# A kernel ordered by a planner gets a new model of its transfer queue, a new table of shifts, and another way to write its last block

## The chip, the cores and the metric

The kernel runs on one core of a Trainium2 chip. The metric is the device time of one execution in microseconds (us). TensorE (PE) does the matmuls, ScalarE (ACT) and VectorE (DVE) the work on vectors, GpSimd (POOL) and SyncE (SP) here mostly issue transfers, which sixteen DMA engines carry out. Each engine works through its own list of instructions in order and waits on semaphores for the others.

## The reference

An attention with cosine-weighted ReLU features, without a softmax, and behind it a two-layer network with a squared ReLU. There are 8 batches, 8 heads, 576 positions and a head size of 64; the network has 512 inputs, 2048 hidden values and 512 outputs.

```
def phi(x, c, s):                       # c, s: cos and sin of pi/2 * position / 576
    r = np.maximum(x, 0.0)
    return np.concatenate([r * c, r * s], axis=-1)
q_p, k_p = phi(q, cos_w, sin_w), phi(k, cos_w, sin_w)
kv  = np.einsum('bhsf,bhsd->bhfd', k_p, v)
num = np.einsum('bhsf,bhfd->bhsd', q_p, kv)
den = np.einsum('bhsf,bhf->bhs', q_p, np.sum(k_p, axis=2))[..., None] + 1e-06
x   = (num / den) -> [8 * 576, 512]
h   = x @ moe_w_in;  r = np.maximum(h, 0.0);  g = r * r
out = g @ moe_w_out                     # float32 [4608, 512]
```

## The kernel before, in words

Of each batch's 576 positions, 512 are worked on as four blocks of 128 (`j` = 0 to 3), and the last 64 are kept as a tail: the tails of all eight batches are put together to a ninth block of 512 rows, which goes through the network last (`b == B`, B = 8).

For a batch `b` the work is this. Two 1 MB loads bring q and k (`ldq`, `ldk`, into `kq`), two of 512 KB v (`ldv`, into `vs`), and small ones the tails (`kqt`, `vst`). ScalarE or VectorE make the features (`cos`, `sin`, into `fe`; of the tails into `fet`, of which there is one buffer). TensorE makes `kz`, the product of features and v. The features of q are transposed: of batches 0 and 1 on TensorE, of the later ones by a DMA transpose on SP's queue (`qTd`: `qpT<-fe` twice and `qpTt<-fet` once for each batch). TensorE makes `num`, VectorE divides (`div`, into `xp`), and the result is transposed again (`xTd`: `xT<-xp` twice and `xTt<-xpt` once). Then come the first layer (`hps` where it is a plain product, in the blocks 0 to 2; `ha`, `hb`, `hc` where it is a product of two by two blocks in seven products P1 to P7 instead of eight, in blocks 3 to 8), the squared ReLU (`rt`, then `gT`), and the second layer (`plan_pair`: `ya`, `yb`, again seven products, with sums `gs` on VectorE; block 0 in `plan_first2`). A store of 512 KB for each half of a block takes it to memory on SP's queue.

The first 17 us are written out by hand (`begin`). All that follows are operations of a planner (`Plan`, lines 133 to 355): each has a cost in us on one engine or on either of ScalarE and VectorE, the operations that it comes after, and the buffers that it holds. `timeline` sets due times along TensorE's work, `dues` carries them back to what it needs, and `run` simulates the engines: at each moment an engine takes the ready operation with the smallest key, which is the due time plus an entry of the table `SHIFT`. `PINS` fixes some operations to one engine. `EARLY`, `EARLY_TAIL`, `STRETCH` and `BIAS` are further settings. The order that comes out is the order in which the instructions are emitted; nothing of the simulation is left at run time, when only the lists and the semaphores count. So whatever changes the planner's figures changes the order on every engine, SP's queue among them.

A transfer ends, for the planner before, by one running time for all transfers (lines 319 to 324), to which a margin `CARE` is added:

```
before, service, behind = o.done
dma = max(dma, free[e] + before) + service
o.end = dma + behind + CARE
```

The last block's second layer (`plan_pair(B, True)`, line 1176 on) has three PSUM buffers of 512 columns: `ya`, `yb` and `yc`. TensorE's order at the end is P1, P5, P6, P3, P7, P2, P4, where P2 adds to `ya` and P4 to `yb`; each is then copied into a half of `y`. The tail block's rows lie in memory in runs of 64, one for each batch. `store` (line 1110) writes one such run from 64 partitions of `y`, 128 KB, and `plan_store` makes eight of these.

## Time and profile before

| | |
|---|---|
| median of 3 runs | 287.29 us (286.31 to 289.38) |
| the profiled execution's own time | 288.8 us |
| span of its instructions | 286.3 us |
| busy: TensorE, VectorE, ScalarE | 269.6, 220.2, 201.0 us |
| granted TensorE clock, mean | 0.986 |
| transfers | 53.0 MB, 185 GB/s over the span |
| last matmul's end; last store's landing; end of the span | 279.6; 285.3; 286.3 us |

The span runs from the first instruction of the profiled execution to its last. A row of a timeline has the start and the length in us, the engine (with a q: its sequencer, which issues transfers), the line, the operation, what it writes and reads, the shapes, how many there were, and in brackets how long the engine had stood idle before it, with what ended that. PEld is TensorE's loading of weights. Lines such as L535 are those of helpers that many operations share, so the tiles tell the work apart.

### The profile page before, as it was taken

How to read it: one execution, taken by the hardware profiler on the slowest of the kernel's cores; microseconds unless marked ns; L12 is line 12 of the kernel's file. 1: busy time of each engine (PE TensorE's matmuls, PEld its weight loads, DVE VectorE, ACT ScalarE, POOL GpSimd, SP SyncE). 2: the span in 40 equal slices, each digit the busy share in tenths (PEclk: the TensorE clock that was granted, in tenths of full speed). 3: DMA queues.
4: the chain of work that ended last, by engine and by line, in shares of the span. 5: the costliest groups of instructions: out<-in, count | busy, mean ns of one | idle time of the engine just before them, and what ended most of it. 6: DMA issues, size and time to landing. Idle time of an engine off the chain costs nothing.

```text
span 286.3 us, 6926 instructions
## 1 busy us (share of the span) xinstructions
PE 269.6 (94%) x2835; PEld 227.5 (79%) x2835; DVE 220.2 (77%) x423; ACT 201.0 (70%) x337; POOL 29.0 (10%) x46
## 2 busy tenths in 40 slices
PE   8999999999979889899988999999999999999990
PEld 3579765888869769788876889988988888888880
DVE  1779658998964988799986997999985956966810
ACT  3769983698398596798559996977675866776510
POOL 8834661100000000000000000000000000000000
PEclk9999999999999999999997999999999999999996
DMA  6999999858999999999994799369511101101106
GB/s 235 310 207 308 319 250 338 269 145 233 342 181 221 262 299 176 294 234 261 242 269 124 185 253 303 137 165 167 36 41 76 74 2 73 76 0 76 72 3 147
DMA packets 77502, 53.00 MB, mean 185 GB/s; under 512 B 52096, under 2 KB 72576, under 8 KB 77472
## 3 DMA queue, kind: packets, MB, share of 16 engines
q1 hardware_dynamic: 70448, 38.81, 55.0%
q0 software_dynamic: 7024, 13.76, 18.4%
q8 instruction: 22, 0.36, 0.6%
q14 instruction: 8, 0.07, 0.1%
HBM read 36.70 MB, written 9.44 MB: 161 GB/s over the span
## 4 chain that ended last, share of the span: by engine, by line
PE 71%; DMA 16%; ACT 4%; SPq 2%; issue 2%; POOL 2%; DVE 1%; POOLq 0%; ACTq 0%
PE ya L535 13%; PE hps L535 12%; PE yb L535 12%; PE hb L535 10%; PE hc L535 6%; PE ha L535 6%; DMA kq<-in_q_dram 5%; PE yh L535 5%; DMA qpT<-fe 4%; DMA kq<-in_k_dram 3%; DMA qpTt<-fet 3%; PE num L535 2%; PE kz L535 2%; SPq L691 1%; ACT fe L522 1%
## 5 line engine op out<-in xcount | busy, mean ns | idle before, releaser
L535 PEld LDWEIGHTS <-w1sb 128*128 128x128 bf16 x800 | 74.1, 98 | 11.1 <-issue 2.5
L516 ACT ACTIVATE gT<-rt 128x512 bf16<-128x512 bf16 x93 | 57.8, 630 | 12.7 <-DVE rt L529 10.2
L535 PEld LDWEIGHTS <-gs 128*128 128x128 bf16 x512 | 50.4, 99 | 8.2 <-issue 1.9
L535 PEld LDWEIGHTS <-gT 128*128 128x128 bf16 x448 | 43.2, 98 | 12.5 <-ACT gT L516 1.5
L535 PE MATMUL hps<-xT,w1sb 128*128 128x256 bf16 (+1 forms) x416 | 45.4, 264 | 1.6 <-DMA xT<-xp 1.6
L522 ACT ACTIVATE fe<-kq,cols 128x1024 bf16<-128x1024 f32 (+1 forms) x35 | 35.1, 1044 | 2.5 <-DMA kq<-in_q_dram 2.0
L535 PE MATMUL ya<-w2sb,gT 128*128 128x256 bf16 x256 | 30.6, 273 | 1.7 <-ACT gT L516 1.3
L535 PEld LDWEIGHTS <-w1s 128*128 128x128 bf16 x288 | 27.6, 98 | 3.8 <-issue 0.6
L524 DVE TENSOR_SCALAR fe<-kq,cols 128x1024 bf16<-128x1024 f32 (+1 forms) x37 | 24.7, 710 | 6.3 <-DMA kq<-in_k_dram 5.4
L535 PE MATMUL hb<-xs,w1sb 128*128 128x256 bf16 x192 | 28.6, 276 | 0.9 <-ACT u L506 0.9
L518 DVE TENSOR_TENSOR gT<-rt 128x512 bf16<-128x512 bf16 x51 | 20.9, 418 | 4.5 <-ACT rt L510 4.2
L535 PE MATMUL ha<-xT,w1sb 128*128 128x256 bf16 x160 | 24.1, 273 | 0.0
L661 DVE TENSOR_TENSOR xp<-num,den 128x512 bf16<-128x512 f32 (+1 forms) x33 | 22.3, 675 | 1.1
L510 ACT ACTIVATE rt<-hps 128x512 bf16<-128x512 f32 x34 | 19.9, 591 | 3.5 <-PE hps L535 2.9
L532 DVE TENSOR_TENSOR gs<-gT 128x2048 bf16<-128x2048 bf16 x16 | 19.5, 1218 | 1.1 <-ACT gT L516 1.0
L529 DVE CUSTOM_DVE_ANT_0 rt<-hb,s 128x512 bf16<-128x512 f32 x24 | 16.4, 684 | 3.1 <-PE hb L535 2.1
L529 DVE CUSTOM_DVE_ANT_0 rt<-hc,u 128x512 bf16<-128x512 f32 x24 | 16.3, 682 | 3.2 <-PE hc L535 3.2
L535 PE MATMUL yb<-w2sb,gs 128*128 128x256 bf16 x128 | 16.3, 284 | 1.6 <-ACT yu L506 1.6
L506 ACT COPY u<-hb 128x512 f32<-128x512 f32 x23 | 13.4, 581 | 4.5 <-PE hb L535 4.5
L506 ACT COPY hb<-ha 128x512 f32<-128x512 f32 x24 | 14.0, 583 | 2.8 <-PE ha L535 1.4
L535 PE MATMUL yb<-w2t,gs 128*128 128x256 bf16 x128 | 15.3, 273 | 0.0
L535 PE MATMUL yb<-w2t,gT 128*128 128x256 bf16 x128 | 15.3, 273 | 0.0
(114 smaller groups left out, 402.4 us busy)
## 6 DMA issues: line engine op xcount, KB each, us to landing
out_dram<-y SPq DMA_DIRECT2D x16, 512.0 KB, 3.4
kq<-in_k_dram SPq DMA_DIRECT2D x6, 1024.0 KB, 6.4
vs<-in_v_dram SPq DMA_DIRECT2D x10, 512.0 KB, 5.3
kq<-in_q_dram SPq DMA_DIRECT2D x5, 1024.0 KB, 6.9
w1sb<-in_moe_w_in_dram POOLq DMA_DIRECT2D x4, 512.0 KB, 10.8
w2sb<-in_moe_w_out_dram POOLq DMA_DIRECT2D x4, 512.0 KB, 10.3
kq<-in_q_dram POOLq DMA_DIRECT2D x2, 1024.0 KB, 11.5
kq<-in_k_dram POOLq DMA_DIRECT2D x2, 1024.0 KB, 10.5
```

The costliest lines, as they stand in the source:

```text
L506: (nc.scalar.copy if e == "ACT" else nc.vector.tensor_copy)(out=out, in_=in_)
L510: nc.scalar.activation(out=out, in_=in_, func=ACTF.Relu)
L516: nc.scalar.activation(out=out, in_=in_, func=ACTF.Square)
L518: nc.vector.tensor_tensor(out=out, in0=in_, in1=in_, op=ALU.mult)
L522: nc.scalar.activation(out=out, in_=in_, func=ACTF.Relu, scale=col)
L524: nc.vector.tensor_scalar(out=out, in0=in_, scalar1=0.0, scalar2=col, op0=ALU.max, op1=ALU.mult)
L529: nc.vector._custom_dve(dve_ops.TENSOR_ADD_SAT, out=out, in0=in0, in1=in1, s0=BIG, s1=0.0)
L532: nc.vector.tensor_tensor(out=out, in0=in0, in1=in1, op=op)
L535: nc.tensor.matmul(out=out, lhsT=lhsT, rhs=rhs, start=start, stop=stop, skip_group_check=True)
L661: nc.vector.tensor_tensor(out=x.rearrange("p (b k) (l d) -> p b k l d", b=n, l=2), in0=n4[:, :, :, 0:D].rearrange("p b (k l) d -> p b k l ...
L691: nc.sync.dma_start_transpose(out=dst, in_=src)
```

## The change

Four things are changed.

The planner's `run` models the transfer queue with a class `Transfers`. An operation now gives the time from its issue to its landing, its service time, and a size, negative for a transpose. The model holds the issuing engine for a big transpose until the transfer ahead has nearly landed, and for other transfers until there is room in a ring of 2500; it adds time where a transpose follows a load, and where a load follows a transpose. `CARE` becomes 1.0, and the landings of the first loads are given 1 to 1.5 us earlier.

The tables `SHIFT` and `PINS` are replaced by shorter ones, and `EARLY`, `STRETCH`, `EARLY_TAIL` and `BIAS` get other values. The order on every engine is another one.

The last block's P2 comes last on TensorE, in two halves of eight matmuls, each into a PSUM buffer of its own of 256 columns (`ya0`, `ya1`), and each with its own copy into `y`. The copy of P1's result into `yb` (the seed) is in two as well.

The last block is stored in four transfers instead of eight. Each takes 128 partitions of `y` to two runs of 64 rows in memory.

```diff
-CARE = 1.5
+CARE = 1.0
+ROOM = 2500
...
-EARLY = 14
-STRETCH = 1.04
-EARLY_TAIL = 15
+EARLY = 20
+STRETCH = 1.08
+EARLY_TAIL = 5
...
-BIAS = 0.3
+BIAS = 0
...
+class Transfers:
+    def __init__(self, at):
+        self.landed, self.turned, self.last, self.out = at, False, 0, []
+
+    def issue(self, end, lat, service, n, ring):
+        size = abs(n)
+        if ring:
+            if n < 0 and self.last >= 512 and self.landed > end - 1.0:
+                self.landed += {2048: 2.0 if self.last > 512 else 0.8, 512: 1.3}.get(size, 0.0)
+            if size >= 2048:
+                end = max(end, self.landed - 0.3)
+            else:
+                self.out = [x for x in self.out if x[0] > end]
+                while sum(x[1] for x in self.out) + size > ROOM:
+                    end = max(end, self.out.pop(0)[0])
+        if n > 0 and self.turned:
+            service += 0.6
+        self.landed = max(end + lat, self.landed + service)
+        self.turned, self.last = n < 0, n
+        if ring:
+            self.out.append((self.landed - 1.5, size))
+        return end, self.landed
...
-                    before, service, behind = o.done
-                    dma = max(dma, free[e] + before) + service
-                    o.end = dma + behind + CARE
+                    free[e], landed = transfers.issue(free[e], *o.done, e == "SP")
+                    o.end = landed + CARE
...
-                offset=((4 * i + 2 * t + g) * S + MAIN) * DM,
-                ap=[[DM, TAIL], [1, DM]],
-            )
-            nc.sync.dma_start(out=dst, in_=y[g * TAIL : (g + 1) * TAIL, t, :])
+                offset=((4 * i + 2 * t) * S + MAIN) * DM,
+                ap=[[S * DM, 2], [DM, TAIL], [1, DM]],
+            )
+            nc.sync.dma_start(out=dst, in_=y[:, t, :])
...
+        for t in range(2) if b == B else [None]:
+            plan_store(b, key, ys[1], 1, [e21, e22], t)
+        for t in range(2 if apart else 0):
+            p2 = prod(2, A, block(0, 1), lambda: w2_block(1, 0), False, seeds, accs[t : t + 1], t, t + 1)
+            e11 = ev(
+                f"c11{t}",
+                flex(1),
+                lambda e, t=t: copy(e, ys[0][:, t, 0:n], A(t)),
+                [p2],
+                [accs[t], ys[0]],
+                0.3,
+            )
+            plan_store(b, key, ys[0], 0, [e11, e12], t)
```

## The prediction

> **What bounds the kernel now.** I read the busy table first, then TensorE's timeline from 17 us on, then the timelines of ScalarE and of SP's queue where TensorE had stood still, then the last 10 us and the DMA view of single stores.

> ```profile
> PE 269.6 (94%) x2835; PEld 227.5 (79%) x2835; DVE 220.2 (77%) x423; ACT 201.0 (70%) x337; POOL 29.0 (10%) x46
> ...
> 81.72 5.40 PE L535 MATMUL hps<-xT,w1sb 128*128 128x256 bf16 x48 [1.56 <-DMA xT<-xp]
> ...
> 100.26 0.32 PE L535 MATMUL num<-kvz,qpTt 128*64 128x65 bf16 x8 [1.01 <-DMA qpTt<-fet]
> ...
> 104.57 1.92 PE L535 MATMUL ya<-w2sb,gT 128*128 128x256 bf16 x16 [1.27 <-ACT gT L516]
> ...
> 116.60 0.60 PE L535 MATMUL hb<-xs,w1sb 128*128 128x256 bf16 x4 [0.89 <-ACT u L506]
> ...
> 151.45 2.97 PE L535 MATMUL yb<-w2sb,gs 128*128 128x256 bf16 x16 [1.57 <-ACT yu L506]
> ```

> TensorE is the bound. Its rows show what a matmul costs when nothing is waited for: sixteen of 256 columns start 1.75 us apart from the next sixteen, so 0.109 us each. From 17.0 us on there are 1,920 of these (209.5 us), 64 of 512 columns at 0.216 (13.8), 64 of 128 columns at 0.056 (3.6), 304 `num` at 0.0306 (9.3), 280 `kz` at 0.032 (9.0) and 86 transposes at 0.053 (4.6): 249.7 us in all. Without a stall TensorE would be through at 266.7. Its last sixteen start at 277.72 and take 1.75, so it ends at 279.5. The stalls are therefore 12.8 us. (The idle figures in the brackets add up to less, because a matmul's end is modelled 0.17 us late.) Start to start, the places are 1.6 us before 81.72, 1.2 before 100.26, 1.4 before 104.57, 1.3 around 116 to 119, and 3.9 between 148.3 and 155, where the clock also fell to half for 3.4 us (sixteen matmuls took 2.97 instead of 1.75). That is 9.4 us. The other 3.4 us lie in pieces under 0.6 us.

> ```profile
> 91.70 0.50 SPq L575 DMA_DIRECT2D kq<-in_q_dram  x1
> 92.30 1.45 SPq L691 DMA_TRANSPOSE qpTt<-fet  x1
> ...
> 109.63 8.11 SPq L691 DMA_TRANSPOSE qpT<-fe  x1
> ...
> 100.24 0.72 ACT L522 ACTIVATE fet<-kqt,cols 128x512 bf16<-128x512 f32 x1 [2.23 <-DMA qpTt<-fet]
> ...
> 115.36 0.72 ACT L522 ACTIVATE fet<-kqt,cols 128x512 bf16<-128x512 f32 x1 [2.22 <-DMA qpTt<-fet]
> ...
> 149.17 0.72 ACT L522 ACTIVATE fet<-kqt,cols 128x512 bf16<-128x512 f32 x1 [2.74 <-issue]
> ```

> All of the 9.4 us come from one cause. A transpose that SP issues behind a 1 MB load lands only after that load: the small `qpTt` of 92.30 lands at 100.2, and the `qpT` of 109.63 holds SP itself for 8.11 us. `fet` has one buffer, so the next batch's `fet` on ScalarE waits for that landing, and everything behind it in ScalarE's order (`gT`, `u`, `yu`) is late for TensorE.

> ```profile
> 277.72 1.91 PE L535 MATMUL yb<-w2t,gT 128*128 128x256 bf16 x16
> 277.92 0.58 ACT L506 COPY y<-ya 128x512 f32<-128x512 f32 x1 [4.66 <-PE ya L535]
> 278.53 5.04 SPq L1125 DMA_DIRECT2D out_dram<-y  x8
> 279.71 0.58 ACT L506 COPY y<-yb 128x512 f32<-128x512 f32 x1 [1.21 <-PE yb L535]
> ...
> DMA packets 144, 0.52 MB, mean 131 GB/s; under 512 B 16, under 2 KB 16, under 8 KB 144
> q1 hardware_dynamic: 144, 0.52, 32.0%
> ...
> DMA packets 640, 1.05 MB, mean 134 GB/s; under 512 B 128, under 2 KB 128, under 8 KB 640
> q1 hardware_dynamic: 640, 1.05, 58.0%
> ```

> The tail is 6.8 us, from 279.5 to the span's 286.3: eviction, the last four of eight stores at 0.62 us each on SP, the last landing at 285.3, and 1.0 us to the end. The DMA lines are of 238 to 242 us (one 512 KB store) and of 278.5 to 286.3 (the eight stores). The first: 128 data packets of 4 KB and 16 tiny ones, which is one per DMA engine. 32.0% of 16 engines in 4 us is 20.5 us, so 0.16 us for a 4 KB packet. The second: eight times 16 tiny ones, and 512 packets of 2 KB, 0.141 us each. So each store, of 64 rows too, is spread over all sixteen engines.

> **The change, part by part.**

> *The order that the planner writes.* No instruction of TensorE goes or comes; 23 of ScalarE's move to VectorE, at some 0.6 us each 14 us, which brings VectorE to 234 of about 272 us: still under TensorE. What moves is SP's queue. Before, the `qpTt` of batch 3 stands directly behind `ldq4`, that of batch 5 behind `ldq6` and `ldk6`, that of batch 4 behind half a v load and a store, and one `qpT` each of batches 3 and 4 directly behind a 1 MB load. In the instruction order of the changed kernel both `qpT` of batches 2 to 5 go out before the next 1 MB load, and the `qpTt` of batches 4 and 5 follow other transposes, those of 2 and 3 half a v load; batch 6 is the exception, with a `qpT` behind `ldk7` and the `qpTt` behind both loads. There are four places to hold TensorE (batch 2's `xT` behind `ldq3`, and the `qpTt` of 3, 4 and 5); I take it that three go and one comes back elsewhere: 9.4 becomes 2.4. Bounds: 0, and 9.4 (all return). The 3.4 us of small pieces stay. TensorE ends at 266.7 + 3.4 + 2.4 = 272.5, bounds 270.1 and 279.5.

> *The last product in two banks.* `P2` goes to the end as two halves of eight matmuls, each with its own eviction. Same matmuls; two evictions of 256 columns (0.37 each, by 0.58 for 512) for one of 512. The seed is split too: 0.16 us more on ScalarE, behind `P7` of pair 7 on TensorE. `P4`, which used to be last, ends 1.75 us before TensorE's end E, and its eviction at E - 0.9, so the first of the four stores goes out at about E - 0.8.

> *The last stores as four.* Each moves 128 partitions x 2 KB, and its destination is no longer one run of 64 rows: it is an outer count of 2 (two batches), then 64 rows. In every transfer of the trace the outermost count is 64 or 128 on both sides, and all sixteen engines take part. No row shows an outermost count of 2 against 128. If a transfer is cut along its outermost count, this one can be cut in two only. Bounds: sixteen engines, as for every row, or two. I take two, because sixteen equal shares of whole outermost entries exist in all the rows and not here. Then an engine carries 64 packets of 2 KB per store, and the four stores queue up on the same two. A packet: 0.141 us by the eight stores, where sixteen engines share 64 partitions; 0.080 by half of a 4 KB packet. The packet records also hold 1 KB at 0.046 and 4 KB at 0.159 (medians of SP's queue), a line that gives 0.084, and the fastest 2 KB packets took 0.081. I take 0.084: here an engine has 64 partitions to itself. 4 x 64 x 0.084 = 21.5 us (bounds 20.5 and 36.1).

> [...]

> *The sum.* First issue E - 0.8; the first packet comes 1.2 us behind an issue of this kind (278.53, packets from 279.75): E + 0.4. Plus 21.5, plus 0.35 to the landing, plus 1.0 to the end: E + 23.3. With E = 272.5 the span is 295.8, against 286.3 (without the edit of the stores, the tail of 6.8 would make it 279.3). The profiled execution took 288.8 around its 286.3, so it would be 298.3; the median shown is 287.29, 1.0 over that span, so I forecast 296.8.

> **The rivals.**

> *Sixteen engines after all (the other side: faster).* For it: every store so far. Against: no row with such a shape. Then only the last store counts: `P2`'s second half ends at E, 0.24 to the eviction, 0.37 for it, 0.1, issue 0.57, 2.2 to the landing (1.75 from issue's end for 64 rows, and four more packets on each engine), 1.0: E + 4.5. That is 277.0, a time of 278.0. It decides as soon as the four stores together take under some 9 us instead of 21.5.

> *Two engines, but another pair for each store.* Then the stores run beside each other: last issue E + 0.7, 1.2, 5.4, 1.35: E + 8.7, span 281.2, time 282.2. For it: nothing in the trace tells one engine from another.

> *Two engines and the slow packet.* 0.141 us makes 36.1 instead of 21.5: 311.4 with E as forecast. For it: it is the only 2 KB row. Against: the fastest of them took 0.081.

> *The order brings nothing.* The stalls move to where the new order has its loads late (the `q` load of a batch is again the last thing before its features), or VectorE at 86% becomes what the evictions wait for. E = 279.5; with two engines 303.8, with sixteen 285.0. For it: a load of 1 MB still takes 6 to 7 us to land, and the q loads come last in both orders.

> **How the numbers follow.** Two engines at about 0.08 to 0.09 us, whatever E: 0.76, from 292 (E 268.5, 0.080) to 304.5 (E 279.5, 0.085). Sixteen: 0.12, mostly at 275 to 282, with a part of 0.02 near 285 to 288. Pairs: 0.04. Slow packet: 0.08, of which a mild one (0.10) ends near 300 to 308. Range 290 to 307. A measurement of this kernel tells about 1% from no change; faster by over 1% 0.14, within 1% 0.03, slower by over 1% 0.83.

> **What would show it.** Right: in the last 25 us TensorE is idle and the DMA engines' share is near 2 of 16 with about 50 GB/s; each of the four stores shows 2 tiny packets instead of 16, and they land some 5.4 us apart; TensorE's last matmul is near 272; no `fet` row on ScalarE is preceded by 2 us for `qpTt` except in batch 7. Wrong: the four stores land within 3 us of their issue (then the time is near 278), or TensorE ends at 279 or later with waits for `kq` or `xT`, or the last landings are 9 us apart.

## The result, and the profile after

The changed kernel takes 300.01 us (median of 4 runs, 297.43 to 301.19); the kernel before, run beside it, 287.85. The ratio is 1.041, with an interval of 1.0312 to 1.0509: slower. Times here and below are medians; the ratios leave disturbed runs out.

The profiled execution has a span of 299.1 us against 286.3, 12.8 more. First the busy table and the clock's row of the page (tenths of full speed in 40 slices of 7.5 us):

```profile
PE 267.7 (90%) x2831; PEld 226.3 (76%) x2835; DVE 230.7 (77%) x451; ACT 185.2 (62%) x311; POOL 28.4 (9%) x46
...
PEclk9999999999999999999999999999999999999655
```

TensorE's busy time is nearly that of before (267.7 us against 269.6); 15.8 us went from ScalarE, 10.5 came to VectorE. The clock is low only in the last three slices, where TensorE has nothing left to do. The timeline of the end says why:

```profile
273.50 1.91 PE L537 MATMUL ya<-w2sb,gT 128*128 128x256 bf16 x16
273.70 0.58 ACT L508 COPY y<-yb 128x512 f32<-128x512 f32 x1 [4.66 <-PE yb L537]
274.31 9.86 SPq L1127 DMA_DIRECT2D out_dram<-y  x4
274.62 0.37 ACT L508 COPY y<-ya 128x256 f32<-128x256 f32 x1 [0.33 <-PE ya L537]
275.45 0.37 ACT L508 COPY y<-ya 128x256 f32<-128x256 f32 x1 [0.46 <-PE ya L537]
```

Sixteen matmuls from 273.50 at 0.109 us end at 275.25, which is 4.2 us earlier than before (279.5). Then 23.85 us pass to the end of the span, instead of 6.8. So the change won 4.2 us and lost 17.05. What runs in that time is in the DMA view of 284 to 294 us, where all four stores have been issued:

```profile
DMA packets 254, 0.51 MB, mean 51 GB/s; under 512 B 4, under 2 KB 4, under 8 KB 254
...
q1 hardware_dynamic: 254, 0.51, 13.1%
```

13.1% of sixteen engines is 2.1 engines. The four tiny packets are two for each of the two stores that end in this window, where before each store had sixteen. By the packet records the 512 packets of 2 KB run from 275.59 to 297.52, each 84 ns (10th to 90th percentile too), and the pairs of tiny ones lie at 282.1, 287.3, 292.4 and 297.5. So the first store takes 6.5 us from its first packet, and each of the others 5.1.

Where TensorE still waits, in the timelines of TensorE and ScalarE, there is no longer 2 us of idle time ahead of a `fet`:

```profile
57.62 1.91 PE L537 MATMUL hps<-xT,w1sb 128*128 128x256 bf16 x16 [0.60 <-ACT rt L512]
...
98.92 0.27 PE L537 MATMUL hps<-xT,w1sb 128*128 128x256 bf16 x1 [0.60 <-DVE xTt L508]
...
123.31 0.42 PE L537 MATMUL num<-kvz,qpT 128*128 128x65 bf16 x8 [1.04 <-DVE xp L663]
...
109.89 1.33 ACT L524 ACTIVATE fet<-kqt,cols 128x512 bf16<-128x512 f32 x2 [0.38 <-DMA qpTt<-fet]
...
156.12 0.72 ACT L524 ACTIVATE fet<-kqt,cols 128x512 bf16<-128x512 f32 x1 [0.86 <-DMA qpTt<-fet]
```

### The profile page after: what moved, and what is told of

Same layout as the page of the kernel before. It is cut to its first block, busy times and chain, and to the rows that moved or that the text cites. A ratio compares the mean times of both kernels' runs of the same rounds, so it can differ in the third digit from the quotient of the medians.

```text
span 299.1 us, 6919 instructions
## 1 busy us (share of the span) xinstructions
PE 267.7 (90%) x2831; PEld 226.3 (76%) x2835; DVE 230.7 (77%) x451; ACT 185.2 (62%) x311; POOL 28.4 (9%) x46
## 4 chain that ended last, share of the span: by engine, by line
PE 55%; DMA 22%; DVE 6%; POOL 3%; ACT 3%; issue 2%; SPq 1%; DVEq 0%; POOLq 0%; ACTq 0%
PE ya L537 15%; DMA kq<-in_q_dram 11%; PE yb L537 11%; PE hb L537 9%; PE hc L537 6%; PE ha L537 6%; PE hps L537 4%; DMA kq<-in_k_dram 4%; DMA w1sb<-in_moe_w_in_dram 4%; PE num L537 2%; DVE fe L526 2%; DMA xT<-xp 2%; PE kz L537 2%; DMA qpTt<-fet 1%; PE yc L537 1%
## 5 line engine op out<-in xcount | busy, mean ns | idle before, releaser
L518 ACT ACTIVATE gT<-rt 128x512 bf16<-128x512 bf16 x77 | 47.4, 628 | 10.3 <-DVE rt L531 5.1
L537 PEld LDWEIGHTS <-gT 128*128 128x128 bf16 x448 | 43.5, 98 | 11.1 <-issue 0.3
L537 PE MATMUL hps<-xT,w1sb 128*128 128x256 bf16 (+1 forms) x416 | 46.1, 264 | 2.0 <-ACT rt L512 1.0
L520 DVE TENSOR_TENSOR gT<-rt 128x512 bf16<-128x512 bf16 x67 | 27.2, 419 | 3.7 <-ACT rt L512 3.0
L537 PE MATMUL hb<-xs,w1sb 128*128 128x256 bf16 x192 | 28.0, 273 | 0.0
L512 ACT ACTIVATE rt<-hps 128x512 bf16<-128x512 f32 x33 | 19.3, 591 | 7.1 <-PE hps L537 7.0
L537 PE MATMUL yb<-w2t,gT 128*128 128x256 bf16 x128 | 15.3, 273 | 0.1
L537 PE MATMUL yb<-w2sb,gs 128*128 128x256 bf16 x128 | 15.3, 273 | 0.0
L537 PE MATMUL yb<-w2t,gs 128*128 128x256 bf16 x128 | 15.3, 273 | 0.0
## 6 DMA issues: line engine op xcount, KB each, us to landing
kq<-in_q_dram POOLq DMA_DIRECT2D x2, 1024.0 KB, 13.1
```

The source lines that it names most:

```text
L512: nc.scalar.activation(out=out, in_=in_, func=ACTF.Relu)
L518: nc.scalar.activation(out=out, in_=in_, func=ACTF.Square)
L520: nc.vector.tensor_tensor(out=out, in0=in_, in1=in_, op=ALU.mult)
L537: nc.tensor.matmul(out=out, lhsT=lhsT, rhs=rhs, start=start, stop=stop, skip_group_check=True)
```

## The experiments

Two questions: what makes the tail 17 us longer, and what made TensorE end earlier. Two measures are used throughout. *Tail* is the span's end less TensorE's end (start of the last sixteen matmuls + 1.75; the last eight + 0.87). *Stalls* are what lies between the starts of TensorE's operations beyond their spacing without a wait, as in the prediction, summed by stage of each kernel's own profile:

| stalls, us | to 60 us | 60 to 90 | 90 to 130 | 130 to 160 | 160 on | ahead of the very last product | all |
|---|---|---|---|---|---|---|---|
| before | 0.8 | 3.1 | 4.3 | 4.0 | 0.6 | 0 | 12.8 |
| after | 2.4 | 0.3 | 2.8 | 0.7 | 1.1 | 0 | 7.3 |
| after, eight stores | 2.1 | 0.4 | 3.4 | 0.7 | 1.5 | 0 | 8.0 |
| order alone | 1.7 | 0.3 | 3.0 | 0.5 | 1.1 | 4.6 | 11.1 |
| order alone, mended | 1.6 | 0.7 | 2.8 | 0.7 | 1.1 | 0 | 6.8 |
| before, five loads moved | 0.8 | 5.4 | 3.7 | 1.1 | 1.6 | 0 | 12.5 |
| before, two loads moved | 1.3 | 3.4 | 2.7 | 3.2 | 0.7 | 0 | 11.3 |
| ... and four features later | 0.9 | 3.8 | 3.9 | 1.5 | 1.7 | 0 | 11.7 |

The traces of after, of the order alone, of the five loads moved and of the four features later hold 61 of the 64 matmuls of 512 columns, all of which start ahead of 60 us; the three without a record are counted as work, 0.65 us. The first kernel and the last two have the same instructions in the same order up to 138 us, and still differ by up to 1.6 us in one stage. A difference below that, from one profile, says nothing.

**The stores, undone.** The change with eight stores of 64 rows:

```diff
-                ap=[[S * DM, 2], [DM, TAIL], [1, DM]],
...
-            nc.sync.dma_start(out=dst, in_=y[:, t, :])
+            for g in range(2):
+                ... offset=((4 * i + 2 * t + g) * S + MAIN) * DM, ap=[[DM, TAIL], [1, DM]],
+                nc.sync.dma_start(out=dst, in_=y[g * TAIL : (g + 1) * TAIL, t, :])
```

> The changed kernel, only the last block's stores as eight again (64 rows each, one run of memory). Theory (an outermost count of 2 leaves two engines): TensorE still ends near 275.2, each store shows 16 tiny packets, the tail is two evictions, two issues of 0.62 us, a landing and the end, about 4.7 us: span 280, time 281, faster than before by some 2%. Rival (the new order or the late second product is what costs): the tail stays above 15 us or TensorE ends later, time above 290.

Measured: 282.22 us, ratio 0.9824 (0.9763 to 0.9884).

```profile
272.48 1.91 PE L537 MATMUL ya<-w2sb,gT 128*128 128x256 bf16 x16
...
273.29 5.05 SPq L1128 DMA_DIRECT2D out_dram<-y  x8
```

TensorE ends at 274.2 and the span at 281.1: a tail of 6.9, as before. Without its stores the change is faster than before, by 5.7 us.

**The stores alone.** The kernel before with the four stores of two runs each (its `g = 1` operations issue nothing):

> The kernel before, only the eight last stores written as four, each to two runs of 64 rows. Theory: TensorE ends at 279.5 as before; the first store's packets start at 279.8 and four times 5.1 to 5.4 us follow on two engines, so the last lands at 300 to 301.5, span 301.5 to 302.5, time 303: 15 to 16 us slower than before. Rival (the slowness belongs to the new order of the last products): within 2 us of before, 286 to 289.

Measured: 304.12 us, ratio 1.0572 (1.0497 to 1.0647).

```profile
278.61 1.91 PE L535 MATMUL yb<-w2t,gT 128*128 128x256 bf16 x16
...
279.43 9.84 SPq L1127 DMA_DIRECT2D out_dram<-y  x4
```

TensorE ends at 280.4, the span at 304.2: a tail of 23.8, with the old order and with P2 in its old place. So the 17 us belong to the stores alone.

**What the count of engines hangs on.** Three runs keep the last 1 MB and cut it differently. The first has four stores of 256 KB each with 64 outermost and the two runs behind. Each reads 64 partitions and both blocks of `y` instead of 128 partitions and one block, so the two stores of the half with the last product wait for both of its evictions:

```diff
-                ap=[[S * DM, 2], [DM, TAIL], [1, DM]],
...
-            nc.sync.dma_start(out=dst, in_=y[:, t, :])
...
+                ap=[[DM, TAIL], [2 * S * DM, 2], [1, DM]],
...
+            nc.sync.dma_start(out=dst, in_=y[g * TAIL : (g + 1) * TAIL, :, :])
```

> The changed kernel with four last stores of the same 256 KB, but each from 64 partitions and both token blocks, so that the outermost count is 64 and the 2 stands behind it; those of the half with the last product wait for both of its evictions. Theory (the outermost count decides): sixteen engines, 16 tiny packets each, tail about 5.2 us, span 280.5, time 281.5. Rival (size, number or the third dimension of the stores decides): as slow as the change, 297 to 301.

Measured: 282.34 us, ratio 0.983 (0.9777 to 0.9884); four issues in 2.92 us, a tail of 5.9.

```profile
272.12 1.91 PE L537 MATMUL ya<-w2sb,gT 128*128 128x256 bf16 x16
...
272.93 2.92 SPq L1128 DMA_DIRECT2D out_dram<-y  x4
```

The number of stores is the same as in the change and the bytes of each too; the 2 has left the outermost place, and 18 us of tail are gone. The source is read another way here, so the other two runs change the destination alone: eight stores of 64 rows, whose destination has an outermost count of 4, or of 16. Both put the 64 rows of a run to memory in another order than the reference has them:

```diff
-                    ap=[[DM, TAIL], [1, DM]],
+                    ap=[[DM, 4], [4 * DM, 16], [1, DM]],      # the other run: [[DM, 16], [16 * DM, 4], [1, DM]]
```

> The changed kernel with eight last stores of 64 rows, the destination written as 4 x 16 rows, which puts the rows of the last block to memory in another order within their run of 64. Theory (as many engines as the outermost count allows): four engines, 4 tiny packets a store, 16 packets of 0.084 us on each, eight stores one behind another 10.8 us: tail 12.5 us, span 287.8, time 289. Rival (only the two runs of memory, or a count of 2, are slow): 16 tiny packets, time 282.

> As the one with an outermost count of 4, but written as 16 x 4 rows, again with the rows of the last block in another order within their run. Theory: sixteen engines, 16 tiny packets a store, time 282 as with eight plain stores. Rival (a third dimension in the destination itself slows a store): 287 or above.

Measured: 290.26 us, ratio 1.0077 (1.0041 to 1.0112), with 4; 283.12 us, ratio 0.9813 (0.9751 to 0.9875), with 16. The DMA view of the first from 277 to 287 us:

```profile
DMA packets 459, 0.88 MB, mean 88 GB/s; under 512 B 28, under 2 KB 28, under 8 KB 459
...
q1 hardware_dynamic: 459, 0.88, 25.8%
```

**Fewer issues at the end.** With sixteen engines, SP's issues are the longest piece of the eight-store tail: 5.05 us from 0.9 us before TensorE's end. To shorten them, this version stores the right half in two of 256 KB and the left one in four of 128 KB, of which the very last, or the last two, are issued by ScalarE:

```diff
+                eng = nc.scalar if not i and t and g else nc.sync        # last two: if not i and t
+                eng.dma_start(out=dst, in_=y[g * TAIL : (g + 1) * TAIL, ts, :])
```

> The changed kernel with the half that is ready first stored as two of 256 KB (outermost count 64), the other as four of 128 KB, the very last of them issued by ScalarE's queue beside SP's. Theory: sixteen engines each, the last two issues side by side, tail about 4.1 us, span 279.3, time 280.3: 0.6 us under the version with eight stores. If issuing from a second queue costs more than it saves, 281 or above.

> The version with the last stores on two queues, with both 128 KB stores of the very last half (instead of one) issued by ScalarE, which is idle by then. There SP's five issues took 3.75 us from 1.1 us before TensorE's end, and the span ended 6.0 us behind TensorE. With four issues on SP (3.0 us) its last landing should come 0.75 us earlier. If the issue time sets the tail: 281.1 us, ratio 0.978. If the packets of both queues share the engines and set it: 281.9 us, ratio 0.981, as with one.

Measured: 281.86 us, ratio 0.9813 (0.9758 to 0.9868), with one on ScalarE; 281.56 us, ratio 0.9794 (0.9745 to 0.9842), with two. Both have a tail of 6.2. With two, SP is done 0.8 us earlier and the last packet still comes 4.5 us behind TensorE's end (4.7 with one). So SP's issues no longer set it; whether the packets or ScalarE's second issue do was not told apart. None of the versions with sixteen engines can be told from another in time.

**The order alone.** After's planner and tables with the last block as before (P4 last, eight stores):

> The planner's part alone: the changed model, tables and settings, but the last block's second layer and its eight stores as before (P2 before P4, one bank, 64 rows each). Theory (the order gains, the late product adds little): TensorE ends near 275.2 instead of 279.5, the tail is the 6.8 us of before, span 282, time 283. Rival (the gain over before belongs to the late product): TensorE ends near 279, time 286 to 288.

Measured: 287.6 us, ratio 1.0005 (0.9966 to 1.0044). The expected gain is missing, and the end of the timeline shows where it went:

```profile
269.43 1.91 PE L537 MATMUL yb<-w2t,gT 128*128 128x256 bf16 x16
...
273.02 0.53 SPq L1120 DMA_DIRECT2D out_dram<-y  x1
275.06 0.69 DVE L534 TENSOR_TENSOR y<-yb,ys 128x512 f32<-128x512 f32 x1 [4.69 <-DMA out_dram<-y]
275.81 3.57 PE L537 MATMUL yb<-w2t,gT 128*128 128x256 bf16 x16 [4.47 <-DVE y L534]
```

The product at 269.43 is pair 7's P4. The new table was made for the other tail, and with the old one it puts this product just ahead of pair 8's last. Pair 7's store then leaves the buffer only at 275, pair 8's sum waits for that buffer, TensorE for the sum, and the last sixteen run at half the clock. Up to there the stalls are 6.5 us, 6.3 less than before. So this run tested not the order, but a clash of the order with a tail that it was not searched for. The same once more, with one entry changed:

```diff
-    "Y7.P4": 15.3,
+    "Y7.P4": -20,
```

> The planner's order alone, once more: as in the run of the order alone, with one entry of the table of shifts changed (pair 7's P4 from 15.3 to -20). In that run's trace the stalls of TensorE up to the last product were 6.95 us against 12.6 before, but pair 7's P4 had been put just ahead of pair 8's P4, so that pair 8's right half waited for the store of pair 7 to leave the buffer: 4.6 us of idle TensorE, then sixteen matmuls at half the clock, 3.57 us instead of 1.91. With pair 7's P4 three products earlier both should go. Theory (the order brings some 5 us, the late product and the stores nothing with eight stores): 287.6 - 4.6 - 1.7 = 281.3 us, between 280 and 283; TensorE ends near 274. Rival (the late product is what frees TensorE's end in the runs with eight stores): no better than 285.5.

Measured: 282.23 us, ratio 0.9803 (0.9757 to 0.9849).

```profile
271.25 1.91 PE L537 MATMUL yb<-w2t,gT 128*128 128x256 bf16 x16
271.45 0.69 DVE L534 TENSOR_TENSOR y<-yc,yu 128x512 f32<-128x512 f32 x1 [1.00 <-PE yc L537]
272.21 5.04 SPq L1127 DMA_DIRECT2D out_dram<-y  x8
```

TensorE ends at 273.0, 6.5 us before the kernel before: 6.0 us of stalls and 0.5 of an earlier start. The tail is 7.0. The order gives the whole gain of about 5 us, and the late product in two banks nothing: 282.22 with it, 282.23 without (the two also differ by that one entry), and the first of the eight stores goes out 0.8 to 0.9 us before TensorE's end in both. Whether the new model, the settings or the table of shifts makes this order the better one was not taken apart.

**Why the old order stalled.** The prediction had one cause: a small transpose behind a 1 MB load. If that were all, moving the loads behind the transposes by hand in SP's list should bring the gain without a planner. Five loads moved (batch 4's q, half of 5's v, 5's q, 6's k and q):

```diff
+        for name, first in (("ldq4", "qTd3.2"), ("ldv5.0", "qTd4.2"), ("ldq5", "qTd4.1"),
+                            ("ldk6", "qTd5.2"), ("ldq6", "qTd5.2")):
+            behind(name, first)          # takes the load out of the order and puts it behind that transpose
```

> The kernel before with five loads moved in SP's list only, each behind a transpose that stood behind it: ldq4 behind the qpTt of batch 3, ldv5.0 and ldq5 behind the qpTt and the second qpT of batch 4, ldk6 and ldq6 behind the qpTt of batch 5. Theory (these holds make the stalls): the waits of ScalarE's fet for qpTt go, and of the 7.6 us of stalls at 100, 104, 116 and 149 some 3 to 6 go, the rest coming back as loads that land 1.5 to 3 us later: time 282 to 285. Rival (the queue is full, an order only moves the wait): 287 to 290.

Measured: 289.5 us, ratio 1.0042 (1.0004 to 1.008). By the time, that theory falls (282 to 285 expected). ScalarE's rows at 100 us:

```profile
100.54 0.71 ACT L522 ACTIVATE fet<-kqt,cols 128x512 bf16<-128x512 f32 x1
102.35 1.15 ACT L522 ACTIVATE fe<-kq,cols 128x1024 bf16<-128x1024 f32 x1 [1.11 <-DMA kq<-in_q_dram]
```

`fet` no longer waits (2.23 us before), as expected. The next row of the same engine now waits for the load that was moved. At 80 us, ahead of every load that was moved, a wait that was 1.56 us before became 2.26, and the clock fell to half behind it:

```profile
82.70 1.65 PE L535 MATMUL hps<-xT,w1sb 128*128 128x256 bf16 x7 [2.26 <-DMA xT<-xp]
```

That is no effect of the move. The run with the four stores alone, which up to there has the list of before, shows the same, 48 matmuls in 7.07 us instead of 5.40:

```profile
82.62 7.07 PE L535 MATMUL hps<-xT,w1sb 128*128 128x256 bf16 x48 [2.14 <-DMA xT<-xp]
```

So the 5.4 us of that stage say nothing against the theory. From 90 to 160 us, where the loads were moved, this profile's stalls are 4.8 us instead of 8.3. What speaks against it is the time, which shows no gain. How often the clock falls at 80 us in either kernel is not known, so one profile does not price the move.

Only the last two of these loads, which had paid in that profile:

> Before, with only two loads moved behind the transposes in SP's order (batch 6's k and q loads behind batch 5's qpTt). In the run with five loads moved, the stall around 148 to 160 us fell from 3.9 to 1.1 us, but others grew by more: 80 to 85 us from 2.4 to 4.8 (with 1.6 of it at half the clock), 100 to 130 us by 2. Theory (a small transpose behind two 1 MB loads is a real wait of TensorE, and moving the loads pays where the features are not soon due): 284.5 us, between 283.5 and 286, ratio 0.990; the stall at 148 to 155 us falls below 1.2 us. Rival (whatever is moved is paid back by a later kq load): 287 us or more, with new waits for kq between 150 and 185 us.

Measured: 289.51 us, ratio 1.0025 (0.998 to 1.007): no gain. ScalarE around 145 us:

```profile
145.00 0.71 ACT L522 ACTIVATE fet<-kqt,cols 128x512 bf16<-128x512 f32 x1
148.15 1.15 ACT L522 ACTIVATE fe<-kq,cols 128x1024 bf16<-128x1024 f32 x1 [2.43 <-issue]
149.20 0.57 ACT L506 COPY yu<-yb 128x512 f32<-128x512 f32 x1
```

The small transpose lands at 139.6 instead of 149.1, and `fet` no longer waits. But the k load lands at 148.07 (147.13 before), nearly as late as the transpose had, and the next row is a feature of that load, with the eviction `yu` behind it. Its releaser is given as "issue", but the row starts 0.08 us behind that landing, and VectorE's features in the same microsecond. TensorE stood still for 2.84 us at 147. So there were two waits in a row for the same 1 MB, and taking one away uncovers the other. In the run with five loads moved, these two among them, the same place looks otherwise:

```profile
148.41 0.72 ACT L522 ACTIVATE fet<-kqt,cols 128x512 bf16<-128x512 f32 x1
149.29 1.15 ACT L522 ACTIVATE fe<-kq,cols 128x1024 bf16<-128x1024 f32 x1 [0.17 <-issue]
```

ScalarE came there 3.4 us later, and the load landed only 1.15 us later (149.22). So the wait depends on how late the engines come: what is saved ahead of this place can be paid back at it, up to the load's landing. Then both at once, by also moving four features behind the evictions next to them:

```diff
+            ("cos6.0", "G4.1.c22q"), ("cos6.1", "G4.1.c22q"),      # ScalarE
+            ("cos6.3", "G4.1.c22r"), ("sin6.1", "G4.1.c22r"),      # VectorE
```

> The run with two loads moved, with four feature rows of batch 6 (two of ScalarE, two of VectorE) moved behind the evictions next to them in their engines' orders, nothing else. There the qpTt of batch 5 landed at 139.6 and fet was no longer waited for, but the k load landed at 148.07, and ScalarE's and VectorE's next rows, features of that load, waited 2.43 and 2.85 us for it, with the evictions u, yu and rt behind them; TensorE stood still for 2.84 us at 146.95. Theory (the root of this stall is a feature row ahead of evictions on an in-order engine before its load has landed; the transpose behind the load was only the first of two such waits): that stall falls below 0.6 us, the profile's TensorE is 2 to 3 us earlier from there on, and the time is 2 to 3 us below that run's (ratio to before about 0.994). Rival (the load is late for everything, and the next user waits as long): the stall moves to kv6 or to batch 6's num near 163 to 170 us, and the time stays at that run's, ratio about 1.003.

Measured: 287.15 us, ratio 1.001 (0.9974 to 1.0045).

```profile
146.41 0.72 ACT L522 ACTIVATE fet<-kqt,cols 128x512 bf16<-128x512 f32 x1
147.02 0.57 ACT L506 COPY yu<-yb 128x512 f32<-128x512 f32 x1
...
148.79 0.60 PE L535 MATMUL hc<-xs,w1s 128*128 128x256 bf16 x4
```

The stall is gone: `yu` follows `fet` without a wait, and so does TensorE. From 130 to 160 us the stalls are 1.5 us, against 4.0 before and 3.2 with the loads alone. The mechanism of this one place is shown by that, in one profile of each kernel. The time did not follow: 1.0 us came back behind 160, the profile's earlier stages happen to stall more, and the ratio is no change within 0.5%. Whether the 1.5 us that are left of the gain are real could not be measured. Whether the same two waits stand at the other three places of before was not tried.

## Why the prediction was right, and where it was not

*Two engines.* Right in the mechanism and in every number that was to show it: 2.1 of 16 engines busy, two tiny packets for each store, 51 GB/s, stores 5.1 us apart (5.4 forecast), 84 ns for a packet (0.084 us forecast), a tail of 23.85 us (23.3). That the packets took 21.9 us in all (21.5 forecast) is partly luck. Past the first store, packets of 84 ns start 80 ns apart on an engine (64 in 5.1 us), where the sum laid them end to end; the first store took 6.5 us, with early packets of up to 0.45 us and gaps, which the sum did not have. The two errors nearly cancel. The guess was argued from what the trace did not hold, a pattern with an outermost count of 2; the runs with 4, 16 and 64 turn it into a row. That all four stores queue up on the same two engines was the author's choice, which no row of before shows; measured are 2.1 busy engines from 284 to 294 us and ends of stores at 282.1, 287.3, 292.4 and 297.5.

*TensorE's end.* Forecast 272.5, measured 275.25, within the bounds, and late by two terms. Its planned work (the first `hps`) began at 18.25 us instead of 17.0; the same order began at 16.5 to 17.3 in the eight other profiles that have it, so that is no effect of the change. (Two of the 86 transposes of its sum start ahead of 17.0, which is 0.1 us.) And the stalls are 7.3 us instead of 5.8; in the mended run of the order alone, with a tail like that of before, they are 6.8. They were to fall by 7.0 us and fell by 5.5, so the size of the gain was nearly right. This late end is most of the 3.2 us by which the forecast of 296.8 lies under the median.

*"All of the 9.4 us come from one cause."* This step failed. It read each wait down to its last releaser, the small transpose, and took the time up to the landing as the price. Behind it in the same engine's order stood a feature that needs the 1 MB load itself, and that lands nearly as late: 148.07 against 149.1 at the place that was taken apart. Moving the loads behind the transposes brought no time, twice. What the new order does at these places, as its trace reads, is both: most transposes go first, and the engine seldom has a row at its head that needs a load still under way. ScalarE's waits ahead of features of batches 3 to 6 are 4.1 us in all, 8.2 before, with 1.4 more ahead of one of batch 2, none before. No run tests this reading by itself. Of the four places, the one at 148 us alone was followed to its cause, and no run that moves loads touched the wait for `xT` ahead of 81.72.

*The late product.* The prediction gave it no gain of its own, and it has none.

*The rivals.* Sixteen engines were to make 278.0. The runs that have them, with the new order, take 281.6 to 283.1. TensorE ends there at 272.8 to 274.9, and the tail of E + 4.5 was too short: with four stores of 256 KB it is 5.9, and with eight at the end 6.8 to 7.0.

## What to carry to other kernels

Before joining stores, look at the outermost count of the destination's pattern: with a count of 2 there 1 MB moved in 22 us instead of 5, and four stores with the 64 outermost cost nothing (a tail of 5.9 us, by 6.9 with eight). A small count in the source was not tried. When a wait is read off a timeline, look at what stands behind the waiting instruction in its own engine's order, and when that could start; the price of the wait is at most what lies between the two (1.0 us at the place that was taken apart, by the landings at 148.07 and 149.1). An order searched for one tail can be wrong for another, so look in the trace of an experiment that undoes one part for what it breaks itself.

## What the runs showed of the hardware

SP is held while it issues stores that pile up on two engines: the third issue took 3.43 us and the fourth 4.97, where the first two took 0.67 and 0.53 (the four make the 9.86 us of the row above).

A 2 KB packet took 84 ns at the median with outermost counts of 2, 4 and 16 in the destination, and in the four stores of 256 KB with 64 outermost. In the eight stores of 64 rows with 64 outermost it took 147 to 149 ns (before, the change with eight stores, the mended order). The tail was 6.9 us with the quick packets (outermost 16) as with the slow ones; SP's issues took 5.13 and 5.05 us there, which fits that they set it. Why the packets are slower was not tried.

TensorE's clock fell to half behind 2.26 us of idle time (82.70, five loads moved) and not behind 2.68 us (at 150.23, two loads moved, where the next sixteen matmuls took 1.91 us). At the same place of the same list, near 82 us, it fell behind 2.14 us (the four stores alone, 48 matmuls in 7.07 us) and not behind 2.24 (four features later, 5.40 us). With the four stores TensorE had been at work again for 1.3 us when the granted clock went to 0.5, at 83.89, for 3.4 us. In the kernel before it was 0.5 from 152.12 to 155.53, that is 3.4 us, from 0.67 us into the work that followed 1.57 us of idle time (151.45). So the length of one gap does not decide it; what does was not shown.
